# Attention score products of a segmented attention block, written in pieces of 128 queries

## The chip, the cores and the metric

The kernel runs on one core of a Trainium2 chip. The metric is the device time of one execution in microseconds (us); of several executions the median is given. The engines that matter here are TensorE (PE, which multiplies matrices; its weight loads are listed as PEld), ScalarE (ACT), VectorE (DVE), GpSimd (POOL) and SyncE (SP, which issues the DMAs). All of them run at the same time and wait for one another through semaphores.

## The reference

The input has 2048 rows of 640. They are normalised, projected to queries, keys and values of 32 heads with 20 channels each, and cut into four segments of 512 rows. Within a segment the attention is causal; a memory `M`, `z` carries sums of earlier segments. A gated unit with 1536 hidden channels works on the same normalised rows, and the output is `x + s * silu(gated unit)`.

```python
for s in range(N):                       # N = 4 segments of L = 512 rows
    qs, ks, vs = (q[:, :, s].copy(), k[:, :, s].copy(), v[:, :, s].copy())
    logits = jnp.einsum('bhqd,bhkd->bhqk', qs, ks) * scale + mask   # causal
    p = _softmax(logits, axis=-1)
    a_dot = jnp.einsum('bhqk,bhkd->bhqd', p, vs)
...
    a_mem = num / den
    o = g * a_mem + (1.0 - g) * a_dot
...
s = _A_ref(xn, A_wq, A_wk, A_wv, A_wo, A_beta)
g = _silu(_B_ref(xn, B_w_gate, B_w_up, B_w_down))
return x + s * g
```

The change touches only the product of queries and keys, `logits`.

## The kernel before, in words

A segment has 32 heads, handled in eight groups of four and those in four pairs of groups. The four heads of a group lie on four strips of 32 partitions: head r has its 20 channels, and four more rows that carry a bound for the exponent, at partitions 32r to 32r+23 of the tiles `QT` and `KT` (`KR` is 24). A score product for head r therefore uses only one strip of 32 rows of TensorE's array, with `tile_position=(32 * r, 0)`, and four such products, one for each head, are issued one after the other on the four strips.

The scores of a causal segment are blocks of 128 keys by 128 queries: 10 of 16 blocks are needed for each head, so 20 for a pair of groups. The table `UNITS` (L43) packs these 20 blocks into five units of four. A unit fills the PSUM tile `Sps` (128 x 4 heads x 512), which exists once. An entry of a unit is `(dg, kb, qb, cnt, c0)`: group within the pair, block of keys, first block of queries, number of query blocks, first column in `Sps`.

- Units 0 and 3 hold the four diagonal blocks of a group: four entries of one block each.
- Units 1 and 4 hold an entry of three blocks (keys 0, queries 1 to 3) and an entry of one block.
- Unit 2 holds two entries of two blocks, one for each group.

`scores` (L576) issues for each entry the four heads' products over all the entry's query blocks at once: pieces of 128, 256 or 384 columns. One exponential on ScalarE (L587) then turns the whole tile into `pt`; in units 0 and 3 GpSimd masks the diagonal blocks afterwards (L591). The next unit's products wait until that exponential has read `Sps`.

The order of all work is made by hand. A loop over 80 slots (four segments, four pairs, five units) issues in each slot the scores of one unit and then fills in projections, gated-unit products and other tasks by the costs and due times in `PLAN`; the value products of a group (`weigh_group`, L625) come ahead of the scores of units 0 and 3. After units 2 and 4 (but for the last pair) the filling products run in a second form (`columns`, L171), as four products of 32 columns of weights each (L176) in place of one of 128 (L179). The planner's costs don't count the products of `scores`, so the order of everything else doesn't depend on how they are cut.

Of the kernel before, what the change touches and what calls it, by code (L numbers as in the profile page):

```python
# [9 lines left out]
P = 128  # L10
# [5 lines left out]
KR = DH + 4  # L16
# [26 lines left out]
UNITS = [  # L43
    [(0, kb, kb, 1, kb * P) for kb in range(4)],
    [(0, 0, 1, 3, 0), (0, 2, 3, 1, 384)],
    [(0, 1, 2, 2, 0), (1, 1, 2, 2, 256)],
    [(1, kb, kb, 1, kb * P) for kb in range(4)],
    [(1, 0, 1, 3, 0), (1, 2, 3, 1, 384)],
]
# [54 lines left out]
def kernel(  # L104
# [14 lines left out]
    nc = tc.nc  # L119
# [218 lines left out]
    def half_tile(tiles, n, half):  # L338
        return tiles[(2 * n + half) % 3]
# [234 lines left out]
    Sps = ps_s.tile([P, 4, L], F32, name="Sps")  # L574

    def scores(n, pair, u):  # L576
        half = pair // 2
        qt, kt = half_tile(QT, n, half), half_tile(KT, n, half)
        for (dg, kb, qb, cnt, c0) in UNITS[u]:
            gi = 2 * pair % 4 + dg  # L580
            for r in range(4):
                nc.tensor.matmul(Sps[:, r, c0:c0 + cnt * P],  # L582
                                 lhsT=kt[32 * r:32 * r + KR, gi, kb * P:(kb + 1) * P],
                                 rhs=qt[32 * r:32 * r + KR, gi, qb * P:(qb + cnt) * P],
                                 start=True, stop=True, tile_position=(32 * r, 0))
        pt = ptp.tile([P, 4, L], BF, name="pt")
        nc.scalar.activation(pt[:], Sps[:], ACT.Exp, scale=SCALE)  # L587
        if u in (0, 3):
            for r in range(4):
                diag = pt[:, r, :].rearrange("p (x c) -> p x c", c=P)  # L590
                nc.gpsimd.affine_select(out=diag, in_=diag, compare_op=ALU.is_ge, fill=0.0, base=0,  # L591
                                        pattern=[[0, 4], [1, P]], channel_multiplier=-1)
        return pt
# [202 lines left out]
    for n in range(NSEG):  # L796
# [46 lines left out]
        for slot in range(NSLOT):  # L843
            pair, u = divmod(slot, NU)
            now = NSLOT * n + slot
            share = max(level - fixed[slot], 0.0)
            if u == 0 and (n or pair):
                q = n * (NG // 2) + pair - 1
                weigh_group(now, q // (NG // 2), q % (NG // 2), 1, pts)
                pts = {}  # L850
            elif u == 3 and not old(n, pair):
                weigh_group(now, n, pair, 0, pts)
            pts[u] = scores(n, pair, u)
            columns[0] = u in (2, NU - 1) and not old(n, pair)
            delay[0] = True
            goal += FIRST * share
            fill(now + 0.45, (tasks,))
            flush()
            for w in due:
                weigh(*w)  # L860
            delay[0] = False
            while first and first[0][0] < now + 1.0:
                run_task(first)
            due = []
            if old(n, pair) and u in (2, 4):
                due.append((n, pair, u // 4, pts))
            goal += (1.0 - FIRST) * share
            fill(now + 1.0, (tasks, soft))
            split()
# [47 lines left out]
```

## Time and profile before

| | |
|---|---|
| median of three runs | 323.56 us (323.13 to 324.31) |
| profiled execution, its own time | 324.77 us |
| span of that execution, first to last instruction | 323.1 us |
| TensorE busy | 312.6 us, 97% of the span |
| ScalarE busy | 244.4 us, 76% |
| VectorE busy | 222.0 us, 69% |
| score products (L582) | 896 |
| exponentials (L587) | 80, 150.5 us in all, 1882 ns each |

The profile's busy time of TensorE counts each product from its start until its result is written; products follow each other faster than that, so the distance from start to start tells what a product costs the engine. The chain that ended last is read from the last instruction back: at each step to whatever released it. A wait is time in which an engine stood idle before an instruction, under the name of what ended the wait.

### The profile page before, as it was taken

Reading aid. Unit: us, or ns where it says so; the run is one execution under the profiler, and the core shown is the slowest. Engines: PE = TensorE matmul, PEld = TensorE weight load, DVE = VectorE, ACT = ScalarE, POOL = GpSimd, SP = SyncE. Lnnn points to the kernel's source line nnn. Section 1 sums busy time; section 2 is a strip of 40 time slices with the busy share of each in tenths; the row PEclk is TensorE's granted clock in tenths of the full one; section 3 lists DMA queues with packets and bytes.
Section 4 is the critical chain, followed back from the end, with each engine's and each line's share of the span. In section 5 each row is a group of like instructions: output and inputs, shape, how many; then the busy total and the mean of one; then the engine's idle time right before and its main releaser. Section 6 shows DMA issues by size and latency. Waiting matters only on the chain.

```text
span 323.1 us, 11284 instructions
## 1 busy us (share of the span) xinstructions
PE 312.6 (97%) x4779; PEld 179.0 (55%) x4808; DVE 222.0 (69%) x523; ACT 244.4 (76%) x275; POOL 127.1 (39%) x228
## 2 busy tenths in 40 slices
PE   7999999899989999999999999999999999999995
PEld 7544555445554565654566465645456655554773
DVE  5476764896669687598977668966756659644445
ACT  7653897798988767687788877676898987798720
POOL 4137323143318123373526533263615352554303
PEclk9999999999999999999999999999999999999999
DMA  7996999944966751443763374233631374230032
GB/s 231 330 285 156 171 209 181 266 129 103 152 141 148 115 126 34 140 120 86 189 111 50 60 120 119 59 115 115 149 79 35 37 143 79 79 82 19 2 65 81
DMA packets 70978, 39.67 MB, mean 123 GB/s; under 512 B 44944, under 2 KB 70928, under 8 KB 70928
## 3 DMA queue, kind: packets, MB, share of 16 engines
q1 hardware_dynamic: 70928, 38.95, 52.1%
q8 instruction: 37, 0.61, 0.9%
q14 instruction: 13, 0.11, 0.1%
HBM read 20.19 MB, written 8.39 MB: 88 GB/s over the span
## 4 chain that ended last, share of the span: by engine, by line
PE 84%; ACT 6%; DMA 3%; DVE 2%; issue 2%; POOL 1%; SPq 0%; ACTq 0%; POOLq 0%
PE gp L179 12%; PE up L179 11%; PE yp L179 9%; PE Sps L582 7%; PE up L176 5%; PE AT L633 5%; PE psv L179 5%; PE psk L179 4%; PE psq L179 4%; ACT pt L587 4%; PE yp L176 3%; PE gp L176 3%; PE sp L176 3%; PE sp L179 3%; PE psq L176 2%
## 5 line engine op out<-in xcount | busy, mean ns | idle before, releaser
L587 ACT ACTIVATE pt<-Sps 128x2048 bf16<-128x2048 f32 x80 | 150.5, 1882 | 23.6 <-PE Sps L582 21.9
L591 POOL TENSOR_SCALAR_AFFINE_SELECT pt<-pt 128x512 bf16<-128x512 bf16 x128 | 81.0, 669 | 154.3 <-ACT pt L587 154.3
L507 DVE SCALAR_TENSOR_TENSOR hT<-hT,up 128x512 bf16<-128x512 bf16 x48 | 32.6, 680 | 26.4 <-PE up L179 11.8
L179 PE MATMUL gp<-xnT,Wg 128*128 128x512 bf16 x174 | 47.0, 380 | 1.4 <-issue 0.8
L179 PE MATMUL up<-xnT,Wu 128*128 128x512 bf16 x164 | 44.0, 380 | 0.6 <-issue 0.5
L179 PE MATMUL yp<-Wd,hT 128*128 128x320 bf16 x265 | 39.2, 299 | 0.0
L496 ACT ACTIVATE hT<-gp 128x512 bf16<-128x512 f32 x48 | 28.8, 599 | 9.3 <-PE gp L179 9.0
L582 PE MATMUL Sps<-QT,KT 24*128 24x128 bf16 (+2 forms) x896 | 31.9, 241 | 1.3 <-ACT pt L587 1.3
L179 PEld LDWEIGHTS <-hT 128*128 128x128 bf16 x265 | 24.7, 98 | 11.9 <-issue 1.9
L526 DVE SCALAR_TENSOR_TENSOR aa<-t,yp 128x320 bf16<-128x320 bf16 x32 | 15.3, 484 | 21.3 <-ACT t L524 21.1
L179 PEld LDWEIGHTS <-Wg 128*128 128x128 bf16 x191 | 17.6, 98 | 19.7 <-issue 1.3
L637 ACT CAST ats<-AT 128x512 bf16<-128x512 f32 x30 | 17.7, 588 | 12.7 <-PE AT L633 12.2
L179 PEld LDWEIGHTS <-Wu 128*128 128x128 bf16 x170 | 15.8, 98 | 18.2 <-issue 1.7
L582 PEld LDWEIGHTS <-KT 24*128 24x128 bf16 x896 | 13.2, 92 | 22.7 <-issue 20.6
L633 PE MATMUL AT<-pt,va 128*32 128x128 bf16 (+1 forms) x840 | 22.4, 242 | 0.2
L633 PEld LDWEIGHTS <-va 128*32 128x32 bf16 x840 | 17.3, 97 | 6.5 <-issue 0.6
L524 ACT ACTIVATE t<-yp 128x320 bf16<-128x320 f32 x32 | 13.9, 439 | 7.0 <-PE yp L179 6.0
L620 DVE TENSOR_TENSOR od<-Asb,rd 128x320 bf16<-128x320 bf16 x30 | 18.5, 616 | 1.0
L563 DVE SCALAR_TENSOR_TENSOR aa<-aa,sp 128x320 bf16<-128x320 bf16 x32 | 15.3, 483 | 5.4 <-PE sp L176 4.1
L533 POOL TENSOR_TENSOR od<-od,om 128x320 bf16<-128x320 bf16 x20 | 17.6, 892 | 2.6 <-DVE od L620 2.6
L176 PE MATMUL up<-xnT,Wu 128*32 128x512 bf16 x280 | 18.5, 381 | 0.0
L179 PE MATMUL psk<-xnT,Wk 128*128 128x512 bf16 x72 | 17.7, 379 | 0.3 <-issue 0.2
(99 smaller groups left out, 465.7 us busy)
## 6 DMA issues: line engine op xcount, KB each, us to landing
KT<-Ks SPq DMA_DIRECT2D x32, 80.0 KB
QT<-Qs SPq DMA_DIRECT2D x32, 80.0 KB
xr<-in_A_x_dram SPq DMA_DIRECT2D x15, 160.0 KB
out_dram<-xr SPq DMA_DIRECT2D x15, 160.0 KB
xt<-in_A_x_dram SPq DMA_DIRECT2D x6, 320.0 KB
Wg<-in_B_w_gate_dram SPq DMA_DIRECT2D x3, 640.0 KB
Wu<-in_B_w_up_dram SPq DMA_DIRECT2D x3, 640.0 KB
Wd<-in_B_w_down_dram SPq DMA_DIRECT2D x4, 480.0 KB
```

The lines of the kernel that those rows point to most:

```text
L176: nc.tensor.matmul(ps[b:b + 32], lhsT=lhsT[:, b:b + 32], rhs=rhs, start=start, stop=stop, tile_position=(0, b), skip_group_check=True)
L179: nc.tensor.matmul(ps, lhsT=lhsT, rhs=rhs, start=start, stop=stop, skip_group_check=True)
L496: nc.scalar.activation(h[:], gp[:], ACT.Tanh, scale=0.5)
L507: empty(lambda: nc.vector.scalar_tensor_tensor(out=h[:], in0=h[:], scalar=1.0, in1=ps[:], op0=ALU.add, op1=ALU.mult), own)
L526: empty(lambda: nc.vector.scalar_tensor_tensor(out=aa[:, hs], in0=t2[:], scalar=1.0, in1=yp[:], op0=ALU.add, op1=ALU.mult), own)
L533: eng.tensor_tensor(o, o, st[n]["om"][:, :, cs], op=ALU.add)
L582: nc.tensor.matmul(Sps[:, r, c0:c0 + cnt * P], lhsT=kt[32 * r:32 * r + KR, gi, kb * P:(kb + 1) * P], rhs=qt[32 * r:32 * r + KR, gi, qb * P ...
L587: nc.scalar.activation(pt[:], Sps[:], ACT.Exp, scale=SCALE)
L591: nc.gpsimd.affine_select(out=diag, in_=diag, compare_op=ALU.is_ge, fill=0.0, base=0, pattern=[[0, 4], [1, P]], channel_multiplier=-1)
L620: nc.vector.tensor_tensor(s["od"][:, :, 4 * g * DH:(4 * g + 4) * DH].rearrange("p q (r e) -> p q r e", e=DH), A[:, :, :, 0:DH], rd[:].unsq ...
L633: nc.tensor.matmul(AT[32 * r:32 * r + 32, qb * P:(qb + cnt) * P], lhsT=v[:, h0:h0 + 32], rhs=pts[u][:, r, c0:c0 + cnt * P], start=(i == 0) ...
L637: nc.scalar.copy(ats[:], AT[:])
```

## The change

Each entry is cut into pieces of one query block. For each piece the four heads' products are issued next to each other, and then the next piece follows. The products' values, their places in `Sps`, the exponential and everything after it stay as they are. Units 0 and 3 already consist of such pieces, so that their instructions are the same as before.

```diff
-        for (dg, kb, qb, cnt, c0) in UNITS[u]:
+        for (dg, kb, q0, cnt, c0) in UNITS[u]:
             gi = 2 * pair % 4 + dg
-            for r in range(4):
-                nc.tensor.matmul(Sps[:, r, c0:c0 + cnt * P],
-                                 lhsT=kt[32 * r:32 * r + KR, gi, kb * P:(kb + 1) * P],
-                                 rhs=qt[32 * r:32 * r + KR, gi, qb * P:(qb + cnt) * P],
-                                 start=True, stop=True, tile_position=(32 * r, 0))
+            for i in range(cnt):
+                for r in range(4):
+                    nc.tensor.matmul(Sps[:, r, c0 + i * P:c0 + (i + 1) * P],
+                                     lhsT=kt[32 * r:32 * r + KR, gi, kb * P:(kb + 1) * P],
+                                     rhs=qt[32 * r:32 * r + KR, gi, (q0 + i) * P:(q0 + i + 1) * P],
+                                     start=True, stop=True, tile_position=(32 * r, 0))
```

## The prediction

> **What bounds the kernel now.** I read the page first, for the engine that carries the end. TensorE is busy nearly all the time at full clock, and the chain of work that ended last is mostly its own:
>
> ```profile
> PE 312.6 (97%) x4779; PEld 179.0 (55%) x4808; DVE 222.0 (69%) x523; ACT 244.4 (76%) x275; POOL 127.1 (39%) x228
> ...
> PEclk9999999999999999999999999999999999999999
> ...
> PE 84%; ACT 6%; DMA 3%; DVE 2%; issue 2%; POOL 1%; SPq 0%; ACTq 0%; POOLq 0%
> ```
>
> So whatever a slot adds to or takes from TensorE goes nearly one to one into the time, and little else does. Next I read who waits around the score products, in the page's groups and in TensorE's waits:
>
> ```profile
> L587 ACT ACTIVATE pt<-Sps 128x2048 bf16<-128x2048 f32 x80 | 150.5, 1882 | 23.6 <-PE Sps L582 21.9
> ...
> L582 PE MATMUL Sps<-QT,KT 24*128 24x128 bf16 (+2 forms) x896 | 31.9, 241 | 1.3 <-ACT pt L587 1.3
> ...
> L582 PEld LDWEIGHTS <-KT 24*128 24x128 bf16 x896 | 13.2, 92 | 22.7 <-issue 20.6
> ```
>
> ```profile
> PE Sps L582 <- ACT pt L587: 1.3, 1, 1.3
> ```
>
> There is one weight load for each of the 896 products. ScalarE waits for scores 33 times (21.9 us in all); TensorE waits for the exponential, the only reader of `Sps`, once, for 1.3 us (the scores that start at 95.50 us). The exponential has slack: in the other slots the scores start 120 ns or more after the exponential before them has ended.
>
> Then I looked at what one unit costs TensorE, in the chain in order of time, where the pieces of all three sizes stand close together (start, length, what):
>
> ```profile
> 98.74 0.33 PE Sps L582 x16
> 99.07 0.32 PE gp L179
> ...
> 102.63 0.33 PE Sps L582 x8
> 102.96 0.97 PE up L179 x4
> ...
> 106.47 0.33 PE Sps L582 x8
> 106.80 0.98 PE gp L176 x16
> ...
> 110.09 0.34 PE Sps L582 x16
> 110.42 0.79 PE psv L179 x5
> ```
>
> x16 is a unit in the form that the change gives to all (units 0 and 3: four pieces of 128 for each of four heads), x8 a unit in the form to be replaced: at 102.63 us 384 and 128, at 106.47 us two of 256. The operands, strips and PSUM tile are of the same kind, and each holds the same 512 columns a head. They take 0.33 to 0.34 us in either form. The reader is to see that the price of the new form is not unknown: it stands in 32 of the 80 slots.
>
> **The change part by part.** It removes, for each pair, 8 products in each of units 1, 2 and 4 and puts 16 in their place: 24 more products and 24 more weight loads a pair, 16 pairs, so 384 of each: 896 becomes 1280. No DMA, no wait and no other engine's instruction is added; the planner's order stays.
>
> *The unit from its first product to the next product that is no score.* I take it from the start times in the trace, which has ns where the timeline rounds to 10 ns. The four products of a set (one piece, four heads) start within 13 ns of each other, so a set is the unit to count.
> Old form, units 1 and 4: 173 ns from the set of 384 to the set of 128, then 156 ns to the next full product (154 when it is one in the column form): 329 or 327 ns. Old form, unit 2: 120 ns, then 207 ns: 327 ns.
> New form, as units 0 and 3 have it: 66, 56 and 56 ns from set to set, then 156 ns: 334 ns. With a product in the column form behind it I take the 154 ns of the old unit's last set, which is a set of 128 too: 332 ns.
> (Twelve units 0 and 3 show 560 ns instead. There a weight load stands without its product, and 560 is 334 plus one product of 512 columns: a missing record, not a cost.)
> So each of the 48 units costs 5 ns more: 48 x 5 = 240 ns. The extra is nearly all the first step of 66 instead of 56 ns and two more steps' rounding.
>
> *The entrance.* A score set behind a product of 512 columns starts 312 ns after that product's start where it is a unit of old form, and also 312 where it is of new form (the first unit 0, at 33.76 us); behind a `yp` product of 320 columns 232 ns in both. Cost of the change: nothing.
>
> *The 384 weight loads.* They run beside the products of the set before, as in units 0 and 3, where the second set's loads start at 43.198 us while the first set's products run from 43.187 to 43.411 us. If that cover were gone, a set would cost what the last set does that nothing follows, 156 ns instead of 56; that is the first rival. What is new to the trace is only that the same weights are loaded again on the same strip, and nothing in the records depends on a weight's value or address, so I take 56 ns.
> The rule that speaks against this is in the Trainium skill, "TensorE: Matmul & The Clock Gate", Part 3, "The mechanism": a weight load overlaps a product in flight only where the row group differs. Here the second set's load on strip 0 has the row group of a product in flight, and yet it starts 11 ns after it, so on these rows the trace does not agree; by the rule the sum would be the first rival's, not 0.24 us.
>
> *Bounds of a unit.* From below: all three steps at the shortest that any shows, 55 ns, and the shortest exit, 153 ns: 318 ns, 9 ns less than now, so 48 x -9 = -0.4 us. From above: all three steps at the longest, 67 ns, and the longest exit, 158 ns: 359 ns, at most 32 ns more than now, so +1.5 us. I take +5 ns, the middle of what 32 units show, and keep both ends for the range.
>
> *The exponential.* It is released when the unit's last product is written: 397 ns after the first in old units, 402 ns in new ones. 5 ns later in an engine that has 24% idle; the smallest slack towards the next scores, 120 ns apart from the one wait, covers it. Cost: nothing beyond the 5 ns already counted. Without that cover it would still be the same 5 ns.
>
> *The issue of 768 more instructions.* TensorE's queue holds products and loads in one order. The densest stretch before issues 128 of them in 1.35 us, 300 in 3.99 us and 400 in 7.89 us; with 16 more in each old unit the same counts would take 1.35, 3.85 and 7.46 us. So rates are asked that lie at most 6% above what is shown. Instruction fetching is 37 transfers, 0.9% of the DMA engines; by the same size each, three more. Cost from below nothing; from above, if each added instruction were paid at the densest rate shown (1.35 us / 128 = 10.6 ns), 768 x 10.6 ns = 8.1 us. I take nothing, because TensorE's gaps that end in its own issue are 53 ns at most, missing records apart, and I keep 8.1 us as a rival.
>
> *What lies off the chain.* From 82.75 to 98.1 us the chain leaves TensorE (transposes, a DMA to `Cs`, ScalarE), and three changed units lie there: their 15 ns may vanish. The chain before and after is TensorE's.
>
> *Sum.* 0.24 us. The profiled execution took 324.77 us, of which 323.1 us are its span and 1.67 us lie around it; it would become 325.01 us. It stands 1.21 us above the median of the three runs, 323.56 us, so the predicted median is 323.8 us.
>
> **The rivals.** About 0.5% (1.6 us) is what a measurement of this kernel can tell from no change.
>
> 1. *Loads on a strip in use are exposed.* Each unit gains two sets, 96 in all; exposed, each costs 156 - 56 = 100 ns more, 9.6 us: 333.4 us, slower. It decides from 17 ns a set on (96 x 17 ns = 1.6 us). For it: nothing in the profile but that weights are loaded twice in a row on one strip. Against it: 32 units with 56 ns from set to set. Chance 0.04.
> 2. *TensorE's issue becomes the bound*, after units 2 and 4 above all, where the column form follows with eight instructions for each product: up to 8.1 us, 331.7 us, slower; from 2.1 ns an added instruction on it decides. Against it: the dense stretches above. Chance 0.05.
> 3. *Short sets follow each other without the step of 66 ns*, because the weights are the same: 318 ns a unit, 323.1 us, no change that can be told. Chance 0.05.
> 4. *The waits shift.* The wait of 1.3 us at 95.50 us, the one of 0.8 us for VectorE's copy of the keys at 58.8 us and the chain of DMAs around them hang on when things are issued. All of TensorE's waits after the start, about 2.5 us, would have to go for a gain over 1.6 us: at best 321.3 us, faster. A shift of 5 ns a slot doesn't do that. Chance 0.03 for a gain over 1.6 us and 0.01 for as large a loss.
>
> **How the numbers follow.** My forecast has 0.82: 323.8 us. Within 0.5%: 0.82 and rival 3, 0.87. Slower: rivals 1 and 2 and the loss of rival 4, 0.10. Faster: 0.03. The range holds the forecast and the bounds of a unit, -0.4 to +1.5 us on 323.56 us, 323.1 to 325.0 us, and 0.2 us more at each end for a median whose runs lie 1.2 us apart: 322.9 to 325.2 us.
>
> **What would show it.** In the profile after: 1280 products and loads in the score line's rows, all with 128 columns; in the chain 0.33 to 0.34 us for x16 in every slot; TensorE's busy share still 97% and full clock; exponentials 1882 ns each with about 22 us of idle time before them. Rival 1 would show as 0.5 us for units 1, 2 and 4 but 0.33 for 0 and 3; rival 2 as TensorE's idle time ending in "issue" behind the column form. The prediction is wrong if a changed unit differs from an unchanged one by more than some 30 ns, or if a wait on TensorE that is not there now exceeds 1 us.

## The result, and the profile after

| | before | changed |
|---|---|---|
| median of 22 runs each | 323.26 us | 324.19 us |
| ratio, 95% interval | | 1.0037 (1.0019 to 1.0055) |
| profiled execution, its own time | 324.77 us | 325.85 us |
| its span | 323.1 us | 324.1 us |

The ratio is not the quotient of the two medians, which is 1.0029. By the ratio the changed kernel is slower by 0.4% (0.6 to 1.8 us by the interval), by the medians 0.93 us. The median is inside the predicted range and the change inside the 0.5% that was called no change, but it is four to five times the 0.24 us that was priced. In two later groups of runs the ratio was 1.0023 (0.9992 to 1.0053) and 1.0024 (1.0000 to 1.0048).

The page of the profile after: TensorE and its instructions, instruction fetching (transfers, MB, share of the DMA engines), and the groups of the exponential and the score products.

```profile
PE 313.2 (97%) x5162; PEld 184.3 (57%) x5192; DVE 222.8 (69%) x523; ACT 244.5 (75%) x275; POOL 126.4 (39%) x228
...
q8 instruction: 40, 0.66, 0.9%
...
L588 ACT ACTIVATE pt<-Sps 128x2048 bf16<-128x2048 f32 x80 | 150.6, 1882 | 25.0 <-PE Sps L583 22.4
...
L583 PE MATMUL Sps<-QT,KT 24*128 24x128 bf16 x1280 | 32.2, 217 | 1.0 <-ACT pt L588 0.9
L583 PEld LDWEIGHTS <-KT 24*128 24x128 bf16 x1280 | 18.6, 92 | 22.3 <-issue 20.7
```

There are 1280 products and loads, all of one shape, and the exponentials and ScalarE's idle time are as before. TensorE's instructions are fetched in 40 transfers instead of 37: 0.66 MB in 40 is 16 KB each, and 768 more instructions brought three more transfers, one for 256. In the trace the fetches lie 177 to 337 of TensorE's recorded instructions apart, some 250 on the mean.

The chain in order of time, at the place that the prediction showed (start, length, what):

```profile
102.51 0.33 PE Sps L583 x16
102.85 0.97 PE up L179 x4
...
106.36 0.33 PE Sps L583 x16
106.69 0.98 PE gp L176 x16
...
109.98 0.33 PE Sps L583 x16
110.31 0.79 PE psv L179 x5
```

Every unit is now x16 and takes 0.33 us. From the first product to the next that is no score, the 48 changed units take 331 to 335 ns in the trace, where 332 and 334 had been worked out. So the extra time is not in the score products. TensorE's waits after the change:

```profile
PE Sps L583 <- ACT pt L588: 0.9, 1, 0.9
...
PE am L179 <- DVE om L482: 0.7, 1, 0.7
PE psk L176 <- DVE k L348: 0.7, 1, 0.7
```

The middle one was not there. The chain shows what stands behind it:

```profile
261.00 0.17 PE am L176 x12
261.17 0.48 PE AT L634 x14
261.65 4.13 DMA Asb<-ats
265.78 0.03 issue
265.80 0.26 DVE rd L618
...
267.66 0.50 DVE om L482
268.16 0.05 issue
268.21 0.34 PE am L179 x3
```

A transposing DMA is issued at 261.65 us and lands 4.13 us later. VectorE waits for it in the division (`rd`), and behind the division stands the evacuation of a memory read (`om`), for which TensorE waits until 268.21 us. In the kernel before, the same transpose, issued at 261.99 us, landed after 2.47 us; its issue (SPq is SyncE's queue) and the division that waits for it are these rows of the timeline:

```profile
261.99 1.19 SPq L640 DMA_TRANSPOSE Asb<-ats  x1
...
264.48 0.25 DVE L617 RECIPROCAL rd<-Asb 128x16 f32<-128x16 bf16 x1 [1.08 <-DMA Asb<-ats]
```

To see where the whole difference lies I subtracted, for each of the 80 units, the distance from the start of its scores to the next unit's in one trace from that in another. Counting what lies ahead of the first unit and behind the last, there are 81 stretches. Ten of them (they end near 34, 43, 61, 66, 95, 99, 122, 201, 267 and 271 us) hold waits behind DMAs and the work around them; they differ by up to 1.3 us between the two profiles of the kernel before, and by up to 3.6 us in other profiles. In the other 71 those two profiles agree within 3 ns. "Price" below is the sum over the 71, against the less disturbed profile of the kernel before (the second, `e1_same`).

### The profile page after: what moved, and what is told of

It is laid out like the page before. It is cut to its first block, busy times and chain, and to the rows that moved or that the text cites. A ratio compares the mean times of both kernels' runs of the same rounds, so it can differ in the third digit from the quotient of the medians.

```text
span 324.1 us, 12051 instructions
## 1 busy us (share of the span) xinstructions
PE 313.2 (97%) x5162; PEld 184.3 (57%) x5192; DVE 222.8 (69%) x523; ACT 244.5 (75%) x275; POOL 126.4 (39%) x228
## 4 chain that ended last, share of the span: by engine, by line
PE 85%; DMA 6%; DVE 4%; ACT 2%; issue 2%; POOL 1%; SPq 0%; ACTq 0%; POOLq 0%; DVEq 0%
PE gp L179 11%; PE up L179 11%; PE yp L179 10%; PE Sps L583 7%; PE psv L179 5%; PE AT L634 5%; PE up L176 5%; PE psk L179 5%; PE psq L179 4%; PE yp L176 4%; PE gp L176 3%; PE sp L176 3%; PE psq L176 2%; PE sp L179 2%; PE psv L176 2%
## 5 line engine op out<-in xcount | busy, mean ns | idle before, releaser
L583 PE MATMUL Sps<-QT,KT 24*128 24x128 bf16 x1280 | 32.2, 217 | 1.0 <-ACT pt L588 0.9
L583 PEld LDWEIGHTS <-KT 24*128 24x128 bf16 x1280 | 18.6, 92 | 22.3 <-issue 20.7
```

What stands on the lines that cost most here:

```text
L583: nc.tensor.matmul(Sps[:, r, c0 + i * P:c0 + (i + 1) * P], lhsT=kt[32 * r:32 * r + KR, gi, kb * P:(kb + 1) * P], rhs=qt[32 * r:32 * r + KR ...
```

## The experiments

The theories. P: the change costs its price of 5 ns a unit and nothing else. W: the shifted score products themselves make waits longer. F, formed after the profiles of the first four runs below: the 768 added instructions move the places at which TensorE's instructions are fetched, and a fetch that meets a transposing DMA delays it.

**The kernel before, again; and the change, again.** No edit in either.

> The kernel before once more, unchanged, against itself. It measures what two groups of runs of one kernel differ by. Theory P (price only: the changed units cost 5 ns each, 0.24 us in all, and the rest of the 0.9 us between the two medians is scatter of the runs) expects that two such groups can differ by 0.5 us or more. Theory W (the shifted score products move waits that end with DMAs, and those cost a repeatable 0.6 us on top) expects a ratio of 1.000 within 0.001. In the profile, the waits of TensorE after the start (about 2.5 us before) should come out within 0.5 us of that for W, and vary by 1 us or more from profile to profile for P.

> The changed kernel once more. Theory P: ratio near 1.0007 (0.24 us), with the waits at 66, 95 and 267 us other than in its first profile. Theory W: ratio 1.003 again (+0.9 us), and the wait of 0.74 us at 268 us (the memory read behind the division that waits for a transposing DMA) there again, because the same shift meets the same DMA.

The kernel before against itself gave 0.9998 (0.9970 to 1.0026), so 0.3% is about what such runs tell apart. Its second profile has a span of 320.5 us, 2.5 us shorter than the first. Its waits of TensorE are all near the start:

```profile
PE wps L669 <- DVE wt L231: 1.0, 1, 1.0
PE cps L402 <- DVE aq L392: 0.3, 1, 0.3
PE pT L329 <- DVE xn L322: 0.2, 1, 0.2
```

The waits for the exponential at 95 us and for the keys at 59 us, which the prediction had taken for a part of this kernel, come in some executions and not in others. (In the profile of "before, division later", below, which is the same program up to there, the one for the exponential is back with 1.1 us, the one for the keys is not.) Neither theory was met: waits vary by 2.5 us from profile to profile, yet medians repeat within 0.15%. The change again gave 1.0023, with a price of 187 ns (183 in its first profile), and the wait near 268 us was there again (0.5 us). In each of its three profiles and in none of the two of before, an instruction fetch starts 0.8 to 1.1 us after the issue of the transpose near 261 us.

**Only unit 2, and only units 1 and 4.**

```diff
-            for i in range(cnt):
+            w = 1 if u == 2 else cnt        # the other kernel: cnt if u == 2 else 1
+            for i in range(0, cnt, w):
...
-                    nc.tensor.matmul(Sps[:, r, c0 + i * P:c0 + (i + 1) * P],
+                    nc.tensor.matmul(Sps[:, r, c0 + i * P:c0 + (i + w) * P],
```

> Only unit 2 is cut (two entries of two blocks become four pieces of 128); units 1 and 4 keep 384 and 128. Price: 16 x 5 ns = 0.08 us. Theory P: 323.3 against 323.26 us, ratio 1.0002. Theory W, if the 0.6 us come from unit 2's shift (it is followed by the column form, as the late places are): ratio 1.002 or more; if they come from the others: 1.000.

> Only units 1 and 4 are cut (384 and 128 become four pieces of 128); unit 2 keeps two of 256. Price: 32 x 5 ns = 0.16 us. Theory P: ratio 1.0005. Theory W: the part of the 0.6 us that unit 2 does not bring, ratio 1.002 to 1.003 if all of it hangs on these units.

Unit 2 alone gave 1.0047 (1.0018 to 1.0076), units 1 and 4 alone 1.0039 (1.0013 to 1.0065). A third or two thirds of the price each, and neither is less slow than the whole: what comes on top is not a sum over units. This speaks against P, and against a W that adds up. In their profiles the transpose near 261 us lands after 2.47 us, and near 268 us TensorE waits no longer than in the first profile of the kernel before (0.34 us for unit 2 alone, nothing for units 1 and 4 alone); they wait elsewhere (2.3 us for a transposed input near 120 us in the one, 1.2 us for the keys and 1.1 us for the exponential in the other).

**Seven units cut, all but seven cut, sixteen cut.** Here the fetches are put in place on purpose. Seven cut units are 112 instructions, and put the fetches from slot 65 on where the whole change has them; sixteen are 256, one whole fetch, and put them back; all but the seven puts them back too.

```diff
-            for i in range(cnt):
+            w = 1 if 49 <= NSLOT * n + NU * pair + u < 60 else cnt    # seven; sixteen: 34 <= ...
+            for i in range(0, cnt, w):                                # all but seven: cnt if ... else 1
```

> Only the seven units 1, 2 and 4 of slots 49 to 59 are cut: 112 instructions of TensorE more ahead of slot 65, which puts its instruction fetches from there on (one of 16 KB for each 256 instructions) where the whole change puts them (39 cut units ahead of slot 65 make 624 = 2 x 256 + 112). Theory F (a fetch that meets a transposing DMA makes it land 1.6 us later, and the change moves the fetches): the transpose of the value product issued near 261 us lands after 3.8 us or more instead of 2.45, and TensorE waits 0.5 to 0.8 us near 268 us, as in the whole change; before slot 49 the fetches lie as in the kernel before; time 0.04 us price + 0.6 us, ratio 1.002. Theory P (the 5 ns a unit are all that the change costs): 7 x 5 ns = 0.04 us, no such wait, ratio 1.000.

> The reverse: all units are cut but those seven. Ahead of slot 65 stand 32 cut units, 512 instructions = 2 x 256, so that from there on the fetches lie as in the kernel before. Theory F: the transpose near 261 us lands after 2.5 us and the wait near 268 us is gone (below 0.3 us); time 41 x 5 ns = 0.2 us of price, and 0.6 us less than the whole change: ratio about 1.001, if no other fetch meets a transpose that matters. A theory by which the 0.6 us come from the later score products themselves (W): the wait at 268 us stays, ratio 1.003.

> The sixteen units 1, 2 and 4 of slots 34 to 59 are cut: 256 instructions of TensorE ahead of slot 65, one whole fetch, so that the fetches from there on lie as in the kernel before. More than twice as many units are cut as in the run of seven. Theory F: the transpose near 261 us lands after 2.45 us, no wait of 0.5 us near 268 us; 16 x 5 ns = 0.08 us, ratio 1.0003. If the number of cut units decides and not the place of the fetches, the wait is there as with seven, ratio 1.002 or more.

Seven units: price 25 ns, ratio 1.0027 (0.9998 to 1.0055). The chain near 261 us is that of the whole change:

```profile
261.00 4.17 DMA Asb<-ats
265.17 0.02 issue
265.19 0.27 DVE rd L619
...
267.11 0.50 DVE om L482
267.61 0.05 issue
267.65 0.34 PE am L179 x3
```

All but seven: price 159 ns, ratio 0.9999 (0.9973 to 1.0026). The chain stays on TensorE throughout, and VectorE's division, in order of time, has its transpose at 263.34 us after 0.55 us of waiting (the transpose was issued at 260.9 us):

```profile
263.34 0.25 DVE L619 RECIPROCAL rd<-Asb 128x16 f32<-128x16 bf16 x1 [0.55 <-DMA Asb<-ats]
```

So fewer cut units give the wait and more don't; the place of the fetch decides, as F had said. Sixteen units: the transpose lands after 2.42 us and the wait near 268 us is gone, also as F had said. But the time did not follow: 1.0018 (1.0000 to 1.0037) where F expected 1.0003. The interval barely holds that, and its median of 324.57 us lies 1.0 us above the kernel before, where the whole change lies too in the same group of runs (324.62 us). F's mechanism was right here and its account of the whole time wasn't.

The transpose near 261 us in all profiles ("wait" is what the two stretches near 267 and 271 us take more than at the least; the last column has the landing counted from the start of the scores of slot 65, near 261 us, which gives TensorE's place in its order):

```
kernel                    fetch starts after issue   landing   wait near 268 us   landed after slot 65's scores began
before                    none near                  2.47 us   0.35 us            2.95 us
before, again             none near                  2.45      0                  2.21
changed                   0.8 us                     4.13      1.14               4.02
changed, again            1.1                        3.85      0.93               3.63
changed, third            0.9                        3.52      0.34               3.34
unit 2 only               none near                  2.47      0.34               2.93
units 1 and 4 only        none near                  2.47      0                  2.59
seven units               0.9                        4.17      0.93               3.75
all but seven             none near                  2.43      0                  2.42
sixteen units             none near                  2.42      0                  2.11
head by head              0.7                        3.59      0.93               3.52
one more set a unit       1.1                        4.40      1.14               4.02
changed, division later   0.8                        3.47      0                  3.62
before, division later    none near                  2.42      0                  1.93
```

Where the division is not moved, the last column alone orders the waits: none up to 2.59 us, 0.34 or 0.35 us from 2.93 to 3.34, 0.93 from 3.52 to 3.75, 1.14 at 4.02 (of which 0.11 us are the two added sets in the run with one more set). So it counts when the transpose lands in TensorE's order, and that has two parts. One is the time from its issue, which a fetch lengthens. The other is the issue itself: in "before" and "unit 2 only" it came 0.5 us after slot 65's scores had begun, where "changed" has it 0.1 to 0.2 us ahead of them, because a transpose of another tile (`oT`) ahead of it in SyncE's queue took 2.4 us to issue where most of these take 1.2 to 1.3; a fetch had started 0.8 and 0.2 us after that one. And in both profiles of the kernel before a fetch meets the next transpose instead: issued 2.5 us after this one, it lands after 3.95 and 4.07 us, and TensorE waits for nothing behind it.

**The division later.** The wait is taken away and the late transpose kept: one division becomes due behind the memory read, and two chunks of TensorE's filling work change places there.

```diff
-        t = now + LAG[2 if last else 1]
+        t = now + LAG[2 if last else 1] + (0.6 if (n, g) == (NSEG - 1, 0) else 0.0)
```

> The whole change, and one division (group 0 of the last segment, which reads the transpose issued near 261 us) due 0.6 slots later, behind the memory read that TensorE waits for near 268 us; at that place one product of the gated unit and one of the output change places. Theory F: the transpose still lands after about 4 us, because the fetch still meets it, but the wait at 268 us is gone (below 0.2 us), and of the whole change's 0.9 us the 0.24 us of price and what other fetches bring stay: ratio 1.001, 0.4 to 0.8 us less than the whole change in the same rounds. Theory W (later score products cost it wherever the division stands): no less than the whole change.

> The same move of one division in the kernel before. Theory F: in the kernel before that transpose lands after 2.45 us and nobody waits long for it, so the move brings 0 to 0.3 us: ratio 0.999 to 1.000. Against the change with the same move it should be about 0.24 us faster, the price alone.

> The changed kernel a third time, beside the three kernels above. Theory F: the transpose near 261 us lands after 3.8 us or more for the third time, TensorE waits 0.5 to 0.8 us near 268 us, ratio 1.002 to 1.004. If the two hits so far were chance, the wait is gone in about half of such profiles.

The change with the division later: 1.0000 (0.9977 to 1.0023), 323.76 us; the change without it, in the same group of runs: 1.0024 (1.0000 to 1.0048), 324.62 us. That is 0.86 us less by the medians, where F had expected 0.4 to 0.8. The transpose still lands late (3.47 us), but the division comes after the memory read and finds it landed, with no wait in brackets:

```profile
263.79 0.49 DVE L482 TENSOR_TENSOR om<-am,rm 128x320 bf16<-128x320 f32 x1
264.88 0.69 DVE L507 SCALAR_TENSOR_TENSOR hT<-hT,up 128x512 bf16<-128x512 bf16 x1 [0.60 <-PE up L179]
265.48 0.25 DVE L618 RECIPROCAL rd<-Asb 128x16 f32<-128x16 bf16 x1
```

The same move in the kernel before gave 1.0001 (0.9975 to 1.0026), also 323.76 us. Between these two even the price can't be seen in the times. The change's third profile met the late transpose for the third time, but with 3.52 us where 3.8 or more were expected, and a wait of 0.34 us where 0.5 or more were: no more than the kernel before has in its first profile. So the 0.86 us between the two medians are not accounted for by the waits of the two profiles beside them.

**Head by head.** The pieces stay, the order is undone.

```diff
-            for i in range(cnt):
-                for r in range(4):
+            for r in range(4):
+                for i in range(cnt):
```

> The pieces of 128 as in the change, but a head's pieces one after the other and then the next head, in place of four heads next to each other. If sets run side by side only because four strips are used in turn, the three pieces of a head follow each other at 56 ns, and only the last piece of a head runs beside the first of the next: an entry of three takes 4 x 2 x 56 + 56 = 504 ns instead of 178, an entry of two 4 x 56 + 56 = 280 instead of 122. Units 1 and 4: +0.33 us each, 32 times, 10.4 us; unit 2: 2 x 0.16 = +0.32 us, 16 times, 5.1 us; together about +15 us, 339 us. If on top a load on the strip in use isn't hidden (rival 1 of the prediction), a piece behind another of its head costs 156 instead of 56 ns: 16 x 16 such pieces in units 1 and 4 (8 each, 256) and 8 in each unit 2 (128) make 38 us more. If the order of the heads makes no difference: 324.2 us.

Measured: 1.0052 (1.0020 to 1.0083), 324.73 us. The two large numbers that were expected (15 us more, and 38 us more on top) were far off. The third, 324.2 us if the order makes no difference, is inside what the interval allows, but the units do differ. A unit 1 or 4 takes 351 to 355 ns instead of 331 to 335, a unit 2 342 to 344 instead of 331 to 334; 10 to 20 ns a unit is all that the neighbourhood of the heads is worth. TensorE's timeline shows a whole unit of two pieces a head for each group:

```profile
257.30 0.42 PE L583 MATMUL Sps<-QT,KT 24*128 24x128 bf16 x16
```

The products' starts in one unit 1 are 0, 10, 20, 30, then 66, 76, 86, 96 ns: four within 30 ns and the next four 66 ns after the first. The records don't name a strip, so whose products these are is inferred. A set on the same strip never follows within less than 55 ns elsewhere, and the distance of the first four goes with the pieces that the program has of one head before the next: 3 to 4 ns in the change (one piece), 7 ns in unit 2 here (two), 10 ns here (three). So the first four are taken to be the first pieces of the four heads, although two more of a head stand ahead of the next head's first in the program.

**One more set.** The price by itself, larger: a set of 128 is written a second time in each of the 48 units.

```diff
+        if u not in (0, 3):
+            for r in range(4):
+                e = c0 + (cnt - 1) * P
+                nc.tensor.matmul(Sps[:, r, e:e + P],
+                                 lhsT=kt[32 * r:32 * r + KR, gi, kb * P:(kb + 1) * P],
+                                 rhs=qt[32 * r:32 * r + KR, gi, (qb + cnt - 1) * P:(qb + cnt) * P],
+                                 start=True, stop=True, tile_position=(32 * r, 0))
```

> The kernel before, with the last set of 128 columns issued a second time in each of the units 1, 2 and 4 (the same values written again): 48 sets on TensorE's path, each priced at 56 ns by the steps of units 0 and 3. Theory P and F: 2.7 us more by price, 326.2 us, ratio 1.008; by F 384 more instructions move the fetches too, which adds between -0.5 and +1 us. If sets behind a loaded strip were hidden in the drain of the set before, less than 1 us.

The chain shows a unit 1, the set added to it, and what follows:

```profile
261.75 0.33 PE Sps L582 x8
262.08 0.06 PE Sps L589 x4
262.13 0.76 PE gp L176 x12
```

55 to 57 ns a unit, 2.7 us by price, as expected. The time went up by 1.5% (1.0082 to 1.0215), 4.7 us by the medians of only four runs (326.32 to 330.88 us), more than the 2.2 to 3.7 us that were expected with the fetches, and with waits of 1.7 us for a transposed input, 1.5 us for the exponential and 0.7 us near 268 us (again with a fetch 1.1 us behind the transpose's issue).

## Why the prediction was right, and which term was mis-sized

*The unit's price* was right. Predicted 5 ns for each of 48 units; in the three profiles of the change the 71 undisturbed stretches, which hold 41 of the units, sum to 183, 187 and 185 ns, so 4.5 ns a unit and 0.22 us in all against 0.24.

*The entrance, the exponential* and *the 384 weight loads* were right: 311 to 313 and 231 or 232 ns behind products of 512 and 320 columns, idle time before the exponentials of 25.0 against 23.6 us, and 55 or 56 ns from set to set in the changed units (65 to 68 for the first step, but 55 in the one unit that had waited for the exponential, near 95 us). Loading the same weights again on one strip costs nothing that a trace shows. Rival 1 is out, and so is rival 3, since the step of 66 ns stays. Head by head goes past what the row of units 0 and 3 could show: by the reading of the starts given there, a strip's products don't wait for those of another strip that stand ahead of them. The Trainium skill, "TensorE: Matmul & The Clock Gate", Part 3, "The mechanism", has products start strictly in the order of the program; by that reading they don't in that run where strips differ.

*The issue of 768 more instructions* is the step that was mis-sized, at nothing. Its bound of 8.1 us looked for the cost on TensorE's own sequencer, and there is none (rival 2 is out: TensorE's waits that end in its own issue are 0.8, 0.5 and 0.2 us before `gp`, `up` and `psk`, as in the kernel before). It noted "three more" fetches and stopped there. What the runs showed in its place is that a transposing DMA lands later when a fetch starts behind its issue, and that adding instructions moves later fetches. One of them came to lie on a transpose that a chain of VectorE and TensorE hangs on. That this place costs 0.34 to 1.14 us in the change's profiles, against the least, is read from the trace (the kernel before has 0 and 0.35 us there). That the fetch brings the late landing and the longer wait is shown by one profile each of four runs: seven units bring them, all but seven and sixteen units lose them, and moving one division loses the wait while the transpose stays late. All but seven and the moved division gave ratios of 0.9999 and 1.0000 where the whole change gave 1.0023 to 1.0037; sixteen units gave 1.0018.

*Rival 4* had the right kind of event and the wrong cause and size. The prediction said that "a shift of 5 ns a slot doesn't do that", which holds, but looked only at shifts of TensorE's time. It also took one profile's waits, 1.3 us and 0.8 us, for the kernel's; the second profile of the same kernel has neither.

What stays open: the times of the partial cuts. Unit 2 alone, units 1 and 4 alone and sixteen units are slower by 0.2 to 0.5%, although in their profiles no fetch meets the transpose near 261 us and TensorE waits near 268 us no longer than before. Other fetches meeting other DMAs are a possible cause, and their profiles do hold such waits, but the kernel before has waits of that kind too, from 0 to 2.5 us by execution, and one profile a kernel can't tell a moved mean from a draw. Nor is it shown that the 0.5 to 1.0 us which the change costs beyond its price, by the ratios of its three groups, lie wholly near 268 us.

## What to carry to other kernels

Where the form that a change introduces already stands in the trace, its price can be read there, and here it held to within a nanosecond a unit. An edit that changes the number of instructions can also move later instruction fetches, as here; on a kernel whose engine is 97% busy, look for transposing DMAs with little slack behind them, and give the reader of such a transpose slack in its own engine's order. And take a second profile of the unchanged kernel before calling a wait its own.

## What the runs showed of the hardware

- TensorE's instructions come in transfers of 16 KB, three more for 768 more instructions. Of the 141 transposes of the value products that are issued after 215 us in the 14 profiles, 33 have a fetch that starts 0.25 to 2.3 us after their issue and landed after 2.61 to 4.46 us (median 3.50); the other 108 landed after 2.40 to 3.32 us (median 2.59). Ahead of 215 us, where the DMA engines are busier (in `e1_same` a share of 0.46 to 0.82 in the stretches up to 200 us, 0.31 from there to 304 us), the two groups overlap widely: 80 with a median of 4.05 us, 199 with one of 2.73 us and single ones up to 5.82 us. Landings are the last of the 16 updates of the DMA's semaphore.
- Four products start within 30 ns of each other even when the program has three of one strip ahead of the next strip's first, which is read here as products of different strips; the order costs 10 to 20 ns a unit of 16.
- Going from a set on strips to a product on the whole array costs about 100 ns: 156 ns from the last set's start instead of 56, and 312 instead of 216 ns on the way in. A unit pays both once, whatever its pieces.
